# Reordering a convolution's transform stage: places of its spectra, an elementwise product, a small copy and two sets of loads

## The chip, the cores and the metric

The kernel runs on one core of one Trainium2 chip. TensorE (PE), VectorE (DVE), ScalarE (ACT) and GpSimd (POOL) compute; SyncE (SP) issues most of the DMAs and ScalarE and GpSimd issue some. The metric is the device time of one execution in microseconds, as a median of several runs.

## The reference

The output holds two computations side by side, in bfloat16. Part A is attention with a memory that runs through 64 segments in sequence; each segment needs the memory rows that the one before it put out:

```python
for s in range(n_seg):                     # 64 segments of 32 rows, D = 1024, 32 heads of 128
    h = jnp.concatenate([mem, xs], axis=1) # 8 memory rows and 32 rows of x
    q, k, v = (einsum('btd,dhe->bhte', h, W) for W in (Wq, Wk, Wv))
    ...
    o = jnp.einsum('bhte,hed->btd', o, Wo)
    mem = o[:, :M, :].copy()
```

Part B is a long convolution of u (2048 rows of 1024 channels) with a kernel K that a state space model gives:

```python
K = jnp.einsum('dn,dnl,dn->dl', Cc, P, dB).real
...
Yf = Uf * Kf                               # transforms of length 4096
y = irfft2(Yf)[..., :L]
y = y + u * Dskip
```

## The kernel before, in words

Part B is computed first (to about 594 us of 1935) and part A after it. Part A needs 512 KB tiles of weights; those that stay in SBUF are loaded while part B still computes, into places that part B has given up, and the others are streamed through a few buffers in every segment.

The changed lines lie in the stage of part B that follows the kernel's construction, the transform. The order of instructions is written out by hand (there is no scheduler): each engine executes its own instructions in program order and waits for others by semaphores. The stage is the loop `for b in range(16)` (L1530). b stands for a quarter of the channels, `dq = b // 4` (256 channels), and one of four blocks of frequencies, `kc = b % 4`. In each iteration:

- `pointwise(b)` (L1458) multiplies the transformed u by the spectrum of K. On DVE: four products `times_u` (L1381, 128x1024 float32; u comes from the buffer wq, the spectrum from PSUM, and the results go to z and back to PSUM), four `rotate` (L1384 and L1385) and the difference `od` (L1471) and sum `y` (L1472). On POOL: the spectra to be inverted, `Bt`, from y (L1474, twice) and from od (L1476 and L1477, on DVE for b = 15). `spectra` (L1454) says in which place of two tiles, Bp with eight places and Bq with four, each goes. Bp's order is the list `stay_` (L1451), which is the fourth row of PLACES.
- `load_u(b + 1)` (L1214) has SP issue the two loads of the next iteration's u into wq (L1216), each of which waits for the products that read that buffer before.
- At b = 3 and from b = 4 on, `load_pair` (L1484) has SP load rows of the plain u (tile uu, 256 KB, four buffers): pair b - 2 in iteration b, and pairs 0 and 1 in b = 3.
- PE computes the next iteration's spectrum (L1225, two halves of 20 matmuls), and behind each half one of the two inverses of pair b - 4 (L1493 to L1525): 16 matmuls of Bt with the inverse matrices MI (L1513), at some places one more with the last tap's rows (L1511), and one with the identity that adds uu (L1525). ACT evicts the sum into uu (L1526) and issues the output DMA (L1498) when both halves are there.
- `skips(n)` (L1488) multiplies uu by D (L1491) in place. That has to be done before L1525 of the same pair. It is called for pair b - 3 on POOL in iterations 3 to 14, behind POOL's spectra, and for pairs 12 to 15 on DVE after the loop.
- SP loads MI in b = 0 to 3 (L1573), in b = 2 the last tap's row, once for each of four partitions and each half of the channels (L1578), and the first rows of u (L1579). Then `next(resident)` issues one load of a part A weight (`residents`, L1674, through L268), as often as a table by b says (L1585). The places and their order are a list of dead tiles.
- At b = 3, `first_state` (L1715) loads the first segment's rows and memory; at the end of b = 10 PE transposes the memory (L1723), DVE copies the result to hT (L1724, 128x64), and POOL copies the rows (L1725).

After the loop come pair 11, three inverses that were begun, and the last eight inverses, pairs 12 to 15. The buffers of MI become free one after another, and weights are loaded into them; part A's first matmuls (L414) follow on PE, with tiles that SP's streaming fetches bring (wst, L340 and L352; a_half, L352).

In the compiled program, DMA issues of SP and ScalarE take eight semaphores in turn, so that an issue waits for the landing of the one eight before it.

Of the kernel before, what the change touches and what calls it, by code (L numbers as in the profile page):

```python
# [690 lines left out]
PLACES = ("e0 o0 e1 o1 e2 o2 e3 o3", "s0 s1 s2 s3 e0 e1 e2 e3", "o0 o1 o2 o3 s0 s2 e0 e2", "s1 s3 e1 e3 o0 o2 s0 e0")  # L691
# [21 lines left out]
def part_b(ctx, tc, u, A_re, A_im, B_re, B_im, C_re, C_im, log_dt, Dskip, out_b, ahead, copies, residents, first_state):  # L713
# [734 lines left out]
    def blocks(t_):  # L1448
        return t_.rearrange("p i c d -> p (i c) d")

    stay_ = PLACES[3].split()  # L1451
    Bp, Bq = (p.tile([128, n_, 2, 2, DQ], BF16, name="Bt", tag="B") for p, n_ in ((bp, 8), (bp0, 4)))

    def spectra(dq, kc, odd_):  # L1454
# [33 lines left out]
    def skips(n_, eng):  # L1488
        d = slice(DQ * (n_ // 4), DQ * (n_ // 4) + DQ)
        uu = held[n_][:].rearrange("p i a d -> p (i a) d")  # L1490
        eng.tensor_tensor(out=uu, in0=uu, in1=Dsk[:, d].unsqueeze(1).to_broadcast([128, 4, DQ]), op=ALU.mult)  # L1491
# [38 lines left out]
    for b in range(16):  # L1530
        points = pointwise(b, now)
        next(points)
        if 0 < b < 15:
            load_u(b + 1)
        for _ in range(4 if b in (2, 3) else 0):
            second.pop(0)()
        if b == 2:
            ks.append([])
        if 2 <= b < 6:
            lo, hi = b - 2, min(b - 1, 3) if b < 5 else 5  # L1540
            ks[1].extend(load_k(1, k1[:, DH * lo:DH * hi], lo))
        if b >= 4:
            load_pair(b - 2, iv)
        if b == 3:
            v.tensor_scalar(out=ident[:], in0=ident[:], scalar1=float(PLEN / 2), scalar2=None, op0=ALU.mult)
            load_pair(0, iv)
            load_pair(1, iv)
            state = first_state(g0[0:8, 5120:6144], iv.tile([128, 8, 24], BF16, name="xt0", bufs=1))
            next(state)
            ctx_k.close()  # L1550
            ps_h = ctx.enter_context(tc.tile_pool(name="b_psh", bufs=1, space=PSUM))
            ps_y = ctx.enter_context(tc.tile_pool(name="b_psy", bufs=2, space=PSUM))
        if b == 0:
            now = nxt_
        elif b + 1 < 16:
            now = []
            for n_ in range(2):
                if b < 3:
                    if n_:
                        next(points, None)  # L1560
                    weighted(b + 1, n_, amps[b + 1])
                now.append(halves(ps_h if b > 2 and (2 * b + n_) % 3 == 0 else ps_e))
                spectrum(b + 1, n_, [now[n_][0][:, half] for half in range(2)])
                if b == 1:
                    make(3, 7)
                if b >= 4:
                    inverses(b - 4, n_)
        next(points, None)
        if 3 <= b < 15:
            skips(b - 3, gp)  # L1570
        if b < 4:
            for i in (2 * b, 2 * b + 1):
                sy.dma_start(out=MI[i][:], in_=MId[2 * i:2 * i + 2].rearrange("c p a k q -> p c a k q"))  # L1573
        if b == 2:
            rows4 = g0[0:4, 5120:6144]
            for i in range(4):
                for half in range(2):
                    sy.dma_start(out=rows4[i:i + 1, DH * half:DH * half + DH], in_=Kx[half][31:32, NF - 1].rearrange("i g c -> i (g c)"))  # L1578
            sy.dma_start(out=w4, in_=u[0:4, :])  # L1579
            gp.tensor_tensor(out=w4, in0=rows4[:, 0:D], in1=w4, op=ALU.mult)  # L1580
            gp.memset(l4, 0.0)
            gp.memset(l4[:, :, 127:128], float(PLEN / 2))
            gp.affine_select(out=l4[:, :, 127:128], in_=l4[:, :, 127:128], compare_op=ALU.is_ge, fill=0.0, base=0, pattern=[[1, 4], [0, 1]],
                             channel_multiplier=-1)
        for _ in range({1: 2, 2: 2, 3: 1, 4: 2, 5: 2, 6: 3, 7: 2, 8: 1, 9: 1, 11: 3, 12: 3, 13: 2, 14: 3, 15: 3}.get(b, 0)):  # L1585
            next(resident)
        if b == 10:
            state.send(ps_y.tile([128, 8, 128], BF16, name="yp", tag="yp")[:, :, 0:8])
# [9 lines left out]
    for _ in range(4):  # L1598
        next(resident)
    for n_ in range(8):  # L1600
        if n_ % 2 == 0:
            skips(12 + n_ // 2, v)
        inverses(12 + n_ // 2, n_ % 2)
        if n_ == 1:
            next(state)
        next(resident)
# [31 lines left out]
@with_exitstack  # L1638
def kernel(
    ctx: ExitStack,  # L1640
    tc: tile.TileContext,
    A_x: bass.AP,
    A_mem0: bass.AP,
    A_Wq: bass.AP,
    A_Wk: bass.AP,
    A_Wv: bass.AP,
    A_Wo: bass.AP,
    A_seg_len: bass.AP,
    B_u: bass.AP,
    B_A_re: bass.AP,  # L1650
    B_A_im: bass.AP,
    B_B_re: bass.AP,
    B_B_im: bass.AP,
    B_C_re: bass.AP,
    B_C_im: bass.AP,
    B_log_dt: bass.AP,
    B_Dskip: bass.AP,
    out: bass.AP,
):
    seg_len = int(A_seg_len)  # L1660
    Dm = A_x.shape[2]
    Db = B_u.shape[2]
    out_a = out[0, :, 0:Dm]
    out_b = out[0, :, Dm:Dm + Db]
    src = weight_blocks(A_Wq.rearrange("d h e -> d (h e)"), A_Wk.rearrange("d h e -> d (h e)"),
                        A_Wv.rearrange("d h e -> d (h e)"), A_Wo.rearrange("h e d -> (h e) d"))
    WD, copies = streamed_copies(ctx, tc, src)
    ahead = Ahead(ctx, tc, A_x[0], src, seg_len)
    ctx_w = ctx.enter_context(ExitStack())
    W_res, places, first = {}, [], {}  # L1670
    rest = Keys(RESIDENT)
    rest.ctx = ahead.ctx = ctx_w

    def residents(stay, early, uqs, last):  # L1674
        def put(t_):
            load_resident(tc, None, src, rest.pop(0), W_res, None, t_)
        for _ in range(EARLY[0]):
            load_resident(tc, stay, src, rest.pop(0), W_res)
            yield
        def some(where, tag, n):  # L1680
            t_ = where.tile([128, n, 2048], BF16, name="W%d" % n, tag=tag)
            return [t_[:, i, :] for i in range(n)]
        for t_ in some(stay, "KT1", 2):
            put(t_)
            yield
        for t_ in early:
            put(t_)
            yield
        put(last[0])
        yield  # L1690
        for t_ in uqs:
            put(t_)
            yield
        ahead.wst = ctx_w.enter_context(tc.tile_pool(name="a_wst", bufs=1, side="right"))
        pool = ctx_w.enter_context(tc.tile_pool(name="a_wre0", bufs=1, side="right"))
        for _ in range(EARLY[1]):
            load_resident(tc, pool, src, rest.pop(0), W_res)
            yield
        for i, key in enumerate([("k", 0, 7)] + streamed_keys()[0:SLOTS - 1]):
            first[key] = t_ = ahead.wst.tile([128, 2048], BF16, name="wst", tag="w%d" % i)  # L1700
            tc.nc.sync.dma_start(out=t_[:], in_=WD[key][:] if key in WD else src(key))
            yield
        for i in [c // 2 for c in PAIRS]:
            places.append(lambda i=i: stay.tile([128, 2048], BF16, name="W1", tag="MI%d" % i))
        for i in range(LATE):
            put(places.pop(0)())
            yield
        put(last[1])
        yield

    low = low_blocks(ctx, tc)
    ahead.low = low.pop()
    copies += [lambda t_=t_: load_resident(tc, None, src, rest.pop(0), W_res, None, t_) for t_ in low]

    def first_state(m0, xt):  # L1715
        nc = tc.nc
        consts = constants(tc, ahead)
        hT = next(consts)
        nc.sync.dma_start(out=xt[:].rearrange("p k r -> p (k r)"), in_=ahead.VXd[0, :, 256:])
        nc.sync.dma_start(out=m0, in_=A_mem0[0])  # L1720
        pm = yield
        for kc in range(8):
            nc.tensor.transpose(out=pm[:, kc, :], in_=m0[:, kc * 128:(kc + 1) * 128], identity=ahead.consts[0][0:8, 0:8])  # L1723
        nc.vector.tensor_copy(out=hT[:, :, ahead.XM:], in_=pm)  # L1724
        nc.gpsimd.tensor_copy(out=hT[:, :, 0:ahead.XM], in_=xt[:])  # L1725
        yield
        next(consts)
        yield

    with ExitStack() as ctx_b:  # L1730
        part_b(ctx_b, tc, B_u[0], B_A_re, B_A_im, B_B_re, B_B_im, B_C_re, B_C_im, B_log_dt, B_Dskip, out_b, ahead, copies, residents, first_state)
    with ExitStack() as ctx_a:
        part_a(ctx_a, tc, A_x[0], src, WD, A_Wo.shape[0] * A_Wo.shape[1], seg_len, out_a, ahead, W_res, rest, places, first)
# [35 lines left out]
```

## Time and profile before

| | us |
|---|---|
| three runs, median (lowest to highest) | 1935.62 (1935.48 to 1936.25) |
| profiled execution, its own time | 1936.64 |
| its span, first to last instruction | 1934.9 |
| part B's transform loop and last inverses | about 407 to 594 of the span |
| PE busy over the span | 1782.2 |
| DVE busy | 1348.0 |
| ACT busy | 918.6 |
| POOL busy | 506.4 |

Rows of the profile name an engine, a line (L12 is line 12 of the kernel), an operation and its tiles as out<-in. A table by windows gives, for each stretch of the span, the busy time of each engine with the number of its instructions, then the granted clock of TensorE (1.00 is full speed), the mean busy share of the 16 DMA engines and the bytes that they moved. A row of waits gives the engine and line that waited, what ended the wait, and total, times and longest. In a list of instructions, [2.56 <-DMA wq<-Ud] is idle time of that engine just before the instruction, with what ended it. SPq and ACTq are the queues in which those engines issue DMAs; a row of the chain that ended last gives start and length of one step.

### The profile page before, as it was taken

Reading aid. Unit: us, or ns where it says so; the run is one execution under the profiler, and the core shown is the slowest. Engines: PE = TensorE matmul, PEld = TensorE weight load, DVE = VectorE, ACT = ScalarE, POOL = GpSimd, SP = SyncE. Lnnn points to the kernel's source line nnn. Section 1 sums busy time; section 2 is a strip of 40 time slices with the busy share of each in tenths; the row PEclk is TensorE's granted clock in tenths of the full one; section 3 lists DMA queues with packets and bytes.
Section 4 is the critical chain, followed back from the end, with each engine's and each line's share of the span. In section 5 each row is a group of like instructions: output and inputs, shape, how many; then the busy total and the mean of one; then the engine's idle time right before and its main releaser. Section 6 shows DMA issues by size and latency. Waiting matters only on the chain.

```text
span 1934.9 us, 73686 instructions
## 1 busy us (share of the span) xinstructions
PE 1782.2 (92%) x31512; PEld 1093.5 (57%) x31563; DVE 1348.0 (70%) x3369; ACT 918.6 (47%) x1654; POOL 506.4 (26%) x897
## 2 busy tenths in 40 slices
PE   8999999877886999999999999999999999999988
PEld 3666666546763555555555555555555555555544
DVE  8599989868992666666766676766666666666650
ACT  8799989940112343444444444434343444444420
POOL 2354545326761111111212121111111111111120
PEclk8999999878997999999999999999999999999999
DMA  7889897858789999999999999999999999999993
GB/s 221 246 235 281 234 286 235 235 171 275 226 290 358 336 346 336 331 346 344 354 347 345 342 352 336 347 344 339 329 352 339 334 344 349 345 334 342 343 336 95
DMA packets 341744, 594.21 MB, mean 307 GB/s; under 512 B 94100, under 2 KB 216476, under 8 KB 339368
## 3 DMA queue, kind: packets, MB, share of 16 engines
q1 hardware_dynamic: 297944, 534.99, 81.1%
q10 hardware_dynamic: 36816, 29.59, 4.7%
q0 software_dynamic: 6656, 24.92, 3.4%
q8 instruction: 247, 4.05, 0.8%
q14 instruction: 81, 0.66, 0.1%
HBM read 531.92 MB, written 71.63 MB: 312 GB/s over the span
## 4 chain that ended last, share of the span: by engine, by line
PE 49%; DMA 29%; DVE 12%; ACT 4%; POOL 3%; issue 3%; SPq 0%; POOLq 0%; DVEq 0%; ACTq 0%
PE acc L414 21%; DMA wst<-WD_v 11%; PE pp L527 9%; DMA wst<-WD_o 8%; DMA arena<-PKd 3%; PE pe L667 3%; DMA wst<-WD_k 3%; PE tr L425 2%; PE pro L184 2%; PE pa L1225 2%; DVE nr L1270 2%; PE pro L197 1%; PE pv L495 1%; POOL uu L1491 1%; PE ptt L1248 1%
## 5 line engine op out<-in xcount | busy, mean ns | idle before, releaser
L414 PEld LDWEIGHTS <-a_hT 128*32 128x32 bf16 x12351 | 331.4, 96 | 323.7 <-issue 75.4
L420 ACT CAST arena<-acc 128x512 bf16<-128x512 f32 x384 | 224.8, 585 | 401.2 <-PE acc L414 333.2
L527 PEld LDWEIGHTS <-arena 128*32 128x32 bf16 x8256 | 215.8, 96 | 77.9 <-issue 56.4
L414 PE MATMUL acc<-wst,a_hT 128*32 128x512 bf16 x2308 | 230.4, 383 | 31.5 <-DMA wst<-WD_v 26.0
L428 POOL COPY arena<-arena 128x128 bf16<-128x128 bf16 x128 | 37.4, 292 | 698.8 <-DMA arena<-PKd 331.4
L335 DVE TENSOR_SCALAR arena<-keep 128x256 int32<-128x256 int32 x508 | 174.3, 395 | 28.1 <-PE acc L414 28.0
L414 PE MATMUL acc<-XM,a_hT 128*32 128x512 bf16 x2560 | 184.2, 380 | 0.0
L414 PE MATMUL acc<-W,a_hT 128*32 128x512 bf16 x1536 | 133.4, 385 | 0.3 <-issue 0.3
L454 DVE TENSOR_REDUCE a_mx<-sc 128x4 f32<-128x160 f32 (+1 forms) x192 | 71.8, 374 | 78.7 <-PE sc L442 78.7
L197 PE MATMUL pro<-XM,wsl 128*128 128x512 bf16 x480 | 117.7, 383 | 5.6 <-DVE kst L206 2.2
L527 PE MATMUL pp<-W_o,arena 128*32 128x256 bf16 x3584 | 121.5, 273 | 0.9 <-issue 0.8
L544 DVE COPY arena<-tr 128x512 bf16<-128x512 bf16 x64 | 27.2, 425 | 125.9 <-PE tr L425 125.9
L458 ACT ACTIVATE sc<-sc 128x160 f32<-128x160 f32 (+1 forms) x192 | 63.9, 333 | 103.5 <-DVE sc L455 102.7
L462 DVE TENSOR_REDUCE a_mx<-sc 128x4 f32<-128x160 f32 (+1 forms) x192 | 72.6, 378 | 55.3 <-ACT sc L458 55.0
L414 PE MATMUL acc<-W_q,a_hT 128*32 128x512 bf16 x1536 | 108.3, 380 | 0.0
L489 POOL TENSOR_TENSOR arena<-arena,a_BD 128x128 bf16<-128x128 bf16 x128 | 51.0, 399 | 216.8 <-DVE arena L472 209.2
L1270 DVE TENSOR_SCALAR nr<-ptt 128x456 f32<-128x456 int16 x128 | 80.3, 628 | 31.4 <-PE ptt L1248 28.6
L1262 ACT ACTIVATE E<-pa 128x648 bf16<-128x648 f32 x128 | 87.7, 712 | 17.7 <-PE pa L1254 15.7
L527 PE MATMUL pp<-wst,arena 128*32 128x256 bf16 x1536 | 76.1, 274 | 18.8 <-DMA wst<-WD_o 16.4
L623 ACT CAST arena<-pp 128x128 bf16<-128x128 f32 x64 | 17.0, 265 | 156.3 <-DVE arena L623 156.3
L513 ACT CAST arena<-pv 128x512 bf16<-128x512 f32 (+1 forms) x128 | 61.3, 479 | 62.9 <-PE pv L499 33.0
L425 PEld LDWEIGHTS <-arena 128*128 128x128 bf16 x1024 | 57.9, 98 | 55.6 <-ACT arena L420 28.9
(332 smaller groups left out, 3961.7 us busy)
## 6 DMA issues: line engine op xcount, KB each, us to landing
wst<-WD_v SPq DMA_DIRECT2D x256, 512.0 KB
wst<-WD_k SPq DMA_DIRECT2D x192, 512.0 KB
wst<-WD_o SPq DMA_DIRECT2D x192, 512.0 KB
wst<-WD_q SPq DMA_DIRECT2D x128, 512.0 KB
Ud<-ux POOLq DMA_DIRECT2D x16, 1024.0 KB, 8.0
wq<-Ud SPq DMA_DIRECT2D x32, 512.0 KB
wsl<-in_A_Wk_dram SPq DMA_DIRECT2D x16, 512.0 KB
wsl<-in_A_Wv_dram SPq DMA_DIRECT2D x16, 512.0 KB
```

The lines of the kernel that those rows point to most:

```text
L197: nc.tensor.matmul(a[:], lhsT=w[:, kc, 128 * j:128 * j + 128], rhs=xTl[:, kc, :, :].rearrange("p s k -> p (s k)"), start=(kc == 0), stop=( ...
L335: nc.vector.tensor_scalar(out=out.bitcast(I32), in0=in_.bitcast(I32), scalar1=0, scalar2=None, op0=ALU.bitwise_or)
L414: nc.tensor.matmul(a[32 * g:32 * g + 32, o_:o_ + rhs.shape[1]], lhsT=hT[:, kc, :], rhs=rhs, start=(kc == 0), stop=(kc == KC - 1), tile_pos ...
L420: nc.scalar.copy(out=q, in_=a[:])
L425: nc.tensor.transpose(out=p[:, hl, :, :].rearrange("p a b -> p (a b)"), in_=q[:, 128 * hl:128 * hl + 128], identity=ident[:])
L454: nc.vector.tensor_reduce(out=m_, in_=x, axis=AX.X, op=ALU.max)
L458: nc.scalar.activation(out=flat(sc, i), in_=flat(sc, i), func=ACT.Exp, scale=scale)
L462: nc.vector.tensor_reduce(out=m_, in_=x, axis=AX.X, op=ALU.add)
L513: copy(out=o[:, i:i + n], in_=p[:, i:i + n, :].rearrange("p a (g q) -> p a g q", g=4))
L527: nc.tensor.matmul(po[32 * qt:32 * qt + 32, o_:o_ + rhs.shape[1]], lhsT=oT[:, h % 4, (h % 16) // 4, :], rhs=rhs, start=False, stop=(h == 3 ...
L1262: sc.activation(out=T["E", r, e // 4][:, lo:lo + 8 * NE].rearrange("p (i c) -> p i c", i=2), in_=T.pop(("p", r, e))[:, :, 0:4 * NE], func= ...
L1270: v.tensor_scalar(out=T["n", r, e // 4][:, lo:lo + 8 * NT], in0=T.pop(("t", r, e))[:, 0:8 * NT].bitcast(I16)[:, 0:16 * NT:2], scalar1=floa ...
```

## The change

The list `stay_` is written out, with s0 two places earlier. `skips` is called for pair b - 2 on POOL in iterations 4 to 14 and for pairs 0 and 1 in iteration 3, so that pair 12 comes to POOL and DVE keeps 13 to 15. The last tap's row is loaded by two DMAs that each write four partitions from one row. The table of kept weights counts 1, 1, 1, 1, 1, 2, 2, 2, 3, 2 for b = 1 to 10 in place of 2, 2, 1, 2, 2, 3, 2, 1, 1, 0, and is the same from 11 on; the tiles and their order are the same. ScalarE copies the state in place of DVE.

```diff
-    stay_ = PLACES[3].split()
+    stay_ = "s1 s3 s0 e3 e1 o0 o2 e0".split()
...
         next(points, None)
-        if 3 <= b < 15:
-            skips(b - 3, gp)
+        for n_ in (0, 1) if b == 3 else (b - 2,) if 3 < b < 15 else ():
+            skips(n_, gp)
...
         if b == 2:
             rows4 = g0[0:4, 5120:6144]
-            for i in range(4):
-                for half in range(2):
-                    sy.dma_start(out=rows4[i:i + 1, DH * half:DH * half + DH], in_=Kx[half][31:32, NF - 1].rearrange("i g c -> i (g c)"))
+            for half in range(2):
+                sy.dma_start(out=rows4[:, DH * half:DH * half + DH], in_=Kx[half][31, NF - 1].rearrange("g c -> (g c)").partition_broadcast(4))
...
-        for _ in range({1: 2, 2: 2, 3: 1, 4: 2, 5: 2, 6: 3, 7: 2, 8: 1, 9: 1, 11: 3, 12: 3, 13: 2, 14: 3, 15: 3}.get(b, 0)):
+        for _ in range({1: 1, 2: 1, 3: 1, 4: 1, 5: 1, 6: 2, 7: 2, 8: 2, 9: 3, 10: 2, 11: 3, 12: 3, 13: 2, 14: 3, 15: 3}.get(b, 0)):
             next(resident)
...
     for n_ in range(8):
-        if n_ % 2 == 0:
+        if n_ > 0 and n_ % 2 == 0:
             skips(12 + n_ // 2, v)
         inverses(12 + n_ // 2, n_ % 2)
...
-        nc.vector.tensor_copy(out=hT[:, :, ahead.XM:], in_=pm)
+        nc.scalar.copy(out=hT[:, :, ahead.XM:], in_=pm)
```

## The prediction

> **What bounds it now.** The edits touch the transform (about 405 to 594 us) and the weight loads that run beside it. I read the stretch in tables by window first, then what each engine waited for between 440 and 595 us, then single instructions.
>
> ```profile
> core 0: us, PE busy (x) PEld busy (x) DVE busy (x) ACT busy (x) POOL busy (x), PEclk, DMA share, GB/s
> 435.00:455.00 20.00, 15.68 (x112) 11.72 (x110) 16.97 (x20) 1.66 (x4) 12.88 (x14) 0.83 0.68 223
> 455.00:475.00 20.00, 15.65 (x120) 12.26 (x118) 17.28 (x20) 1.79 (x3) 10.12 (x7) 0.91 0.97 313
> 475.00:515.00 40.00, 34.61 (x296) 28.92 (x300) 39.31 (x43) 4.78 (x8) 29.44 (x22) 1.00 0.86 277
> 515.00:535.00 20.00, 17.39 (x154) 14.25 (x154) 16.96 (x20) 2.39 (x4) 13.10 (x11) 1.00 0.56 166
> 535.00:575.00 40.00, 32.07 (x263) 26.06 (x266) 38.96 (x42) 4.78 (x8) 28.35 (x21) 0.97 0.92 306
> 575.00:595.00 20.00, 19.21 (x161) 14.12 (x165) 5.74 (x6) 5.35 (x9) 12.29 (x46) 0.97 0.84 281
> 595.00:640.00 45.00, 28.73 (x517) 15.38 (x513) 16.82 (x48) 11.53 (x24) 3.09 (x9) 0.77 1.00 362
> ```
>
> DVE is busy 39.31 of 40 us and 38.96 of 40 us in two of these rows; POOL is not (29.44). From 595 on DMA is (share 1.00). So VectorE sets the pace up to its last product at 575 us, then PE's last inverses, then the transfers. What DVE waits for is short, and it is nearly all there is to win:
>
> ```profile
> DVE z L1381 <- DMA wq<-Ud: 4.9, 2, 2.6
> DVE a_hT L1724 <- PE yp L1723: 2.7, 1, 2.7
> DVE uu L1491 <- DMA uu<-in_B_u_dram: 1.4, 1, 1.4
> DVE od L1471 <- POOL uu L1491: 0.5, 1, 0.5
> ```
>
> The columns are total, times, longest. PE's own list for 440 to 640 us begins otherwise:
>
> ```profile
> PE yp L1525 <- POOL uu L1491: 17.8, 11, 3.6
> PE acc L414 <- DMA a_half<-in_A_Wq_dram: 11.0, 1, 11.0
> ```
>
> The 17.8 us is the idle time at which "u times D two inverses ahead" aims. In a steady iteration it is cover, not cost: two first products of DVE, one iteration apart, stand 9.65 us apart, and DVE has no gap between them:
>
> ```profile
> 503.93 1.21 DVE L1381 TENSOR_TENSOR z<-wq,pa 128x1024 f32<-128x1024 f32 x1
> ...
> 513.58 1.21 DVE L1381 TENSOR_TENSOR z<-wq,pa 128x1024 f32<-128x1024 f32 x1
> ```
>
> **The change part by part.**
>
> *Order of the spectra's places.* The same eight names in the same tile, another index. The instructions and what they wait for stay; no engine gets or loses one. 0, and I see no way to a loss but a changed overlap with weights that are loaded into that tile's place at the end, which come after the last inverse in both. 0 to +0.3.
>
> *Tap rows by two loads, and weights later, before b=4.* SyncE issues these one after another in b=2 and 3:
>
> ```profile
> 439.83 5.69 SPq L1578 DMA_DIRECT2D g<-Kx  x8
> ...
> 446.27 0.43 SPq L268 DMA_DIRECT2D W_q<-in_A_Wq_dram  x1
> 446.80 1.04 SPq L1216 DMA_DIRECT2D wq<-Ud  x2
> ```
>
> DVE's instructions around that load, and the loads themselves in the chain that ended last:
>
> ```profile
> 441.71 1.22 DVE L1381 TENSOR_TENSOR pa<-wq,pa 128x1024 f32<-128x1024 f32 x1
> ...
> 449.44 1.22 DVE L1472 TENSOR_TENSOR y<-y,pa 128x1024 f32<-128x1024 f32 x1
> 453.22 1.22 DVE L1381 TENSOR_TENSOR z<-wq,pa 128x1024 f32<-128x1024 f32 x1 [2.56 <-DMA wq<-Ud]
> ...
> 461.74 1.22 DVE L1472 TENSOR_TENSOR y<-y,pa 128x1024 f32<-128x1024 f32 x1
> ```
> ```profile
> 446.80 6.33 DMA wq<-Ud
> ...
> 457.71 7.54 DMA wq<-Ud
> ```
>
> Eight tap rows hold SP for 5.69 us (0.71 each); two hold it for about 1.4. One of the two weights behind them goes too (0.4 with its gap). So SP reaches the load of u (L1216) at about 442.1, and then waits for the product that still reads its buffer, which ends at 441.71+1.22 = 442.93. It is issued 3.85 us earlier. With an unchanged 6.33 us it lands at 449.3, before DVE is free at 449.44+1.22 = 450.66. The 2.56 us go. The second half (issued at 447.3, and now about 446.65, behind b=3's second product) is wanted 2.26 us after the first; one weight fewer ahead of it, 512 KB or 1.45 us at the 362 GB/s of the last window row, makes it timely; if that helps nothing it costs 0.85 again. **−2.56 (−1.7 to −2.56).**
>
> *The same, b=5.* The second wait (4.9 less 2.56) ends with the load issued at 457.71, which took 7.54 and landed at 465.25; DVE had been free since 461.74+1.22 = 462.96. With the first wait gone that is 460.4. SP comes there earlier too, at about 454.5 (−3.2: it loses the first delay and one more weight), so 0.65 is won with the same duration, and up to all 2.38 if two weights fewer (three before b=4 instead of five; 2.9 us at 362 GB/s) shorten the 7.54 fully. They don't: the kept queue is full only in part of that time (share 0.97 for 455 to 475), and MI and W_q stay ahead. I take the middle, **−1.6 (0 to −2.38)**, leaving 0.8 of wait.
>
> *Weights moved to b=6 to 10.* Counts 3,2,1,1,0 become 2,2,2,3,2: the same 16 by b=10. In b=9 (from 503.93) and 10 (from 513.58) the queue then carries 5 tiles instead of 1, 2.1 MB more, 5.8 us at 362 GB/s, in stretches whose shares are 0.86 and 0.56, which leave 5.6 and 8.8 us. Iterations with three tiles exist already (b=11, 12, 14) and lie in the row with share 0.92, where DVE stays at 38.96 of 40 us. **0; if one load of u came late there, about +2.5, like the two waits above.**
>
> *State's copy on ScalarE.* DVE's instruction waits in order for PE's transposes:
>
> ```profile
> 522.08 1.22 DVE L1472 TENSOR_TENSOR y<-y,pa 128x1024 f32<-128x1024 f32 x1
> 526.00 0.19 DVE L1724 COPY a_hT<-yp 128x64 bf16<-128x64 bf16 x1 [2.69 <-PE yp L1723]
> 526.10 1.21 DVE L1381 TENSOR_TENSOR z<-wq,pa 128x1024 f32<-128x1024 f32 x1
> ```
>
> Without it the product starts at 522.08+1.22 = 523.30 instead of 526.10: **−2.8**. Next late would be its PSUM input from PE or the second half of u. PE has 17.39 of 20 us in that window, so its spectrum can be the next wait, at most some tenths: −2.2 to −2.8. ScalarE takes the copy beside 2.39 us of work in 20; behind it wait one eviction and one output DMA, by 2.7 us at most, which no product of DVE needs. 0.
>
> *u times D earlier.* POOL gets one more, of DVE's four, and does two in b=3:
>
> ```profile
> L1491 POOL TENSOR_TENSOR uu<-uu,Dsk x12: 2116/2127/2136, 457.5 to 570.2; 128x1024 bf16<-128x1024 bf16 x12
> ```
> ```profile
> 490.06 0.38 SPq L1486 DMA_DIRECT2D uu<-in_B_u_dram  x1
> ```
> ```profile
> 457.51 2.13 POOL L1491 TENSOR_TENSOR uu<-uu,Dsk 128x1024 bf16<-128x1024 bf16 x1 [1.54 <-DMA uu<-in_B_u_dram]
> ...
> 494.44 2.50 POOL L1474 TENSOR_TENSOR Bt<-y 128x512 bf16<-128x512 f32 x2 [2.53 <-DVE y L1472]
> ...
> 499.36 2.14 POOL L1491 TENSOR_TENSOR uu<-uu,Dsk 128x1024 bf16<-128x1024 bf16 x1
> ```
>
> The extra 2.13 us on POOL in b=3 stand in its idle time before b=4's spectra; 0. In the loop POOL's place for it does not move, but it takes the pair whose load was issued in the same iteration: 490.06 to 499.36 is 9.3 us for a load for which POOL waited once already (at 457.51). PE's 17.8 us vanish; DVE gains of them only the wait of 0.5 at b=13 (taken 0, −0.5 to +0.3).
>
> In the tail they count, since DVE is done:
>
> ```profile
> 572.35 0.38 PE L1525 MATMUL yp<-uu,b_ident 128*128 128x512 bf16 x1 [3.11 <-POOL uu L1491]
> ```
> ```profile
> 574.84 3.32 POOL L1474 TENSOR_TENSOR Bt<-y 128x512 bf16<-128x512 f32 x2 [2.54 <-DVE y L1472]
> ```
> ```profile
> 599.96 8.70 DMA a_half<-in_A_Wq_dram
> ```
>
> PE comes to its last eight inverses 3.11 earlier, but cannot pass POOL's last spectra (578.16); I count 2.3 us. Of these little arrives: the next part waits 11.0 us for a_half, whose 8.70 us in a full queue follow an issue by SP, and SP stood before a weight load for most of this:
>
> ```profile
> SPq L268 <- DMA out_dram<-uu: 10.4, 2, 9.0
> ```
>
> In this program an issue from SP or ScalarE waits for the landing of the one eight issues before it, whose semaphore it takes; here that was an output. After it, landings are set by the bytes queued since DVE's end, which move with DVE. **−0.8 (0 to −4.6)** for the part of PE's 2.3 that frees W1's places and outputs sooner.
>
> **Sum.** −2.56 −1.6 −2.8 −0.8 = −7.8 us against the profiled run (span 1934.9, 1936.64 with what lies around it): 1928.8. The median of three is 1.02 lower, so **1927.8**. It carries to the end because DMA is full from 595 on, and moving the start of a full queue moves its end.
>
> **Rivals.**
>
> 1. *The queue is the bound already.* If the transform's loads fill the time, an earlier DVE only meets a later load. For it: shares of 0.97, 0.92, 0.84. Against: 0.56 and 0.86 leave 14 us before 535, and the weights by b=10 are as many in both. It would leave the first wait's saving and little else: −3, 1932.6.
> 2. *Loads of u stay late.* b=5 keeps its 2.38 (−6.2, 1929.4), and one of the refilled iterations gets a wait of 2.5: −3.7, 1931.9.
> 3. *The tail carries through.* If outputs land sooner, SP's 9.0 us of waiting shortens, and with it the idle share of DMA before 595 (0.84 of 20 us, 3.2 us idle): 2.3 more, up to 4.6: 1923.2 to 1925.5. Against: the 9.0 us are one output's, with SP's queue full beside it, and that queue is as full in the changed kernel. The Trainium skill (DMA: Bandwidth & Descriptors, Queues, rings and completion order) says that each DMA engine takes packets in turn from the queue rows that have work, so that ScalarE's output should not wait behind all of SP's transfers; by that rule the time would be this rival's. The trace does not agree with it, by those 9.0 us.
> 4. *PE's chain is the truth.* All 17.8 us go: −18 and the rest, 1917 or less. Against: DVE has no gap in a steady iteration.
> 5. *Slower: the load of the pair comes too late for POOL.* POOL does its work in order; u times D stands ahead of the next spectra, which free od and y for DVE. It is asked 9.3 us after issue; POOL then has 2.5 us of idle time (the wait at 494.44). DVE's next od gives another 2.2: it starts 7.25 after its iteration's first product (522.08−1.25−513.58), so at 501.5 in the iteration that began at 494.3, when POOL had read the last od by 499.36. From 14.0 us of transfer on, each us more costs 1 us in each of 11 iterations; at 15.1 that is 11.7: +3.9, 1939.5. Against: 7.54 and 8.70 are the long transfers of these rows.
>
> **How the numbers follow.** Forecast 0.52 (its own range 1925.3 to 1929.9, half of the way from the terms taken to the sums of their ends, −3.6 and −12.8), rival 1: 0.11, rival 2: 0.15 (a third of it the later waits), rival 3: 0.14, rival 4: 0.03, rival 5: 0.05. 0.2%, about what a measurement of this kernel can tell from no change, is 3.9 us: below 1931.75 is faster. Rival 1 and a third of rival 2 are within it: 0.16; slower 0.05; faster 0.79. The range 1923.2 to 1932.7 leaves out rivals 4 and 5 and the edges of 1 and 3, under 0.2.
>
> **What would show it.** In the profile after: DVE's list without L1724 and with 0.8 us or less before L1381; PE's 17.8 us for L1491 gone, without any change of DVE's 9.65 us; first product of b=15 about 7 us earlier; a_half landing about 8 us earlier; the rest of the program shifted alike. Wrong it is if POOL waits for DMA before L1491 in the loop, if L1381 waits for wq at b=10 to 15, or if a_half's landing moves by much less than DVE's end.

## The result, and the profile after

The changed kernel takes 1927.82 us in the median of 16 runs (1918.85 to 1939.08), the kernel before 1934.3 in 16 runs beside it (1926.73 to 1942.21). The ratio is 0.9963, with a 95% interval of 0.9947 to 0.998: 7.2 us less, from 3.9 to 10.3. The forecast was 1927.8, 7.8 us below the 1935.62 of the first three runs before.

From lowest to highest the executions of one kernel lie 15 to 20 us apart, so the parts can't be read from times. They can be read from one profile each, since the loop's steps repeat within some hundredths of a microsecond. The profiled execution after has a span of 1924.1 us (its own time is 1925.86). The windows of before, in the changed kernel (columns as there):

```profile
475.00:515.00 40.00, 36.49 (x315) 30.23 (x314) 39.31 (x42) 4.78 (x8) 29.61 (x22) 1.00 0.87 277
515.00:535.00 20.00, 18.63 (x164) 15.05 (x163) 19.66 (x22) 2.49 (x5) 15.08 (x12) 1.00 0.92 305
535.00:575.00 40.00, 34.14 (x278) 27.08 (x277) 37.66 (x40) 6.11 (x11) 29.16 (x32) 0.97 0.90 289
575.00:595.00 20.00, 14.58 (x148) 9.93 (x146) 1.98 (x3) 4.04 (x7) 6.20 (x32) 0.93 1.00 351
```

The third busy time is DVE's: the hole of b = 11 (16.96 of 20 us before) is closed, 19.66. From 475 to 515 DVE is as full as before; from 535 to 575 it has 37.66 in place of 38.96, since its last y now comes 6 us earlier. DMA's share from 575 to 595, 0.84 before, is 1.00. The waits of DVE in the loop and the tail (total, times, longest):

```profile
DVE z L1381 <- DMA wq<-Ud: 2.2, 1, 2.2
DVE uu L1491 <- issue: 1.0, 1, 1.0
DVE uu L1491 <- DMA uu<-in_B_u_dram: 0.8, 1, 0.8
```

One of two waits for u has stayed, nearly whole; L1724 and od at b = 13 are gone. Of PE's waits, 440 to 640 us, these are the ones to compare:

```profile
PE acc L414 <- DMA a_half<-in_A_Wq_dram: 10.7, 1, 10.7
PE pa L1225 <- DVE y L1385: 9.1, 10, 1.6
...
PE yp L1525 <- POOL uu L1491: 0.2, 1, 0.2
```

17.8 us of waiting for u times D became 0.2, and the waiting for DVE (L1385), which frees the PSUM that the spectrum is written to, grew from 1.8 to 9.1.

To cut the stretch into parts I use three starts of DVE's last instruction of an iteration, L1472 (y of b = 2, 5 and 15), and the first matmul that waits for a_half. Before, then after; the last row of each is PE's:

```profile
438.58 1.22 DVE L1472 TENSOR_TENSOR y<-y,pa 128x1024 f32<-128x1024 f32 x1
...
473.85 1.22 DVE L1472 TENSOR_TENSOR y<-y,pa 128x1024 f32<-128x1024 f32 x1
...
573.54 1.22 DVE L1472 TENSOR_TENSOR y<-y,pa 128x1024 f32<-128x1024 f32 x1
...
608.70 0.61 PE L414 MATMUL acc<-a_half,a_hT 128*32 128x512 bf16 x2 [10.96 <-DMA a_half<-in_A_Wq_dram]
```
```profile
438.53 1.22 DVE L1472 TENSOR_TENSOR y<-y,pa 128x1024 f32<-128x1024 f32 x1
...
471.02 1.22 DVE L1472 TENSOR_TENSOR y<-y,pa 128x1024 f32<-128x1024 f32 x1
...
567.48 1.22 DVE L1472 TENSOR_TENSOR y<-y,pa 128x1024 f32<-128x1024 f32 x1
...
600.32 0.61 PE L414 MATMUL acc<-a_half,a_hT 128*32 128x512 bf16 x2 [10.74 <-DMA a_half<-in_A_Wq_dram]
```

The differences in us, with the same rows of each experiment's profile (one profile each; E6, E7 and E11 were also timed in 10 or 12 runs):

| kernel | y2 to y5 | y5 to y15 | y15 to a_half | sum |
|---|---|---|---|---|
| before | 35.27 | 99.69 | 35.16 | 170.12 |
| changed | 32.49 | 96.46 | 32.84 | 161.79 |
| E1: before, copy on ScalarE | 35.38 | 96.46 | 35.45 | 167.29 |
| E2: before, two tap loads | 32.69 | 99.67 | 35.68 | 168.04 |
| E3: before, new table of weights | 33.36 | 99.67 | 35.44 | 168.47 |
| E4: before, u times D earlier | 35.93 | 98.04 | 33.17 | 167.14 |
| E5: changed, old order of places | 32.60 | 96.46 | 32.94 | 162.00 |
| E6: changed, two MI later | 30.16 | 96.45 | 32.90 | 159.51 |
| E7: changed, pairs loaded last | 32.99 | 96.46 | 33.59 | 163.04 |
| E8: changed, u times D late | 32.50 | 96.46 | 35.61 | 164.57 |
| E9: before, outputs held | 35.31 | 101.15 | 33.17 | 169.63 |
| E10: changed, outputs held | 32.89 | 96.46 | 31.45 | 160.80 |
| E11: changed, MI later, outputs held | 31.91 | 96.46 | 32.14 | 160.51 |
| E12: changed, old table of weights | 33.16 | 96.44 | 33.37 | 162.97 |

The change moved 8.33 us in this stretch: 2.78, 3.23 and 2.32. What follows a_half, 1326.2 us before (1934.9 less 608.70) and 1323.8 after, holds the same instructions in both, and in these 14 profiles it varies from 1319.6 (E2) to 1329.6 (E11) without order. The y of b = 2 stands at 436.93 (E4) to 442.44 (E9). These two are the spread of the times.

### The profile page after: what moved, and what is told of

Its sections match the earlier page's. It is cut to its first block, busy times and chain, and to the rows that moved or that the text cites. A ratio compares the mean times of both kernels' runs of the same rounds, so it can differ in the third digit from the quotient of the medians.

```text
span 1924.1 us, 73734 instructions
## 1 busy us (share of the span) xinstructions
PE 1779.6 (92%) x31563; PEld 1091.4 (57%) x31563; DVE 1346.2 (70%) x3367; ACT 919.5 (48%) x1655; POOL 508.2 (26%) x898
## 4 chain that ended last, share of the span: by engine, by line
PE 45%; DMA 32%; DVE 14%; ACT 4%; issue 3%; POOL 2%; SPq 1%; DVEq 0%; POOLq 0%; ACTq 0%
PE acc L414 21%; DMA wst<-WD_v 12%; PE pp L527 8%; DMA wst<-WD_o 8%; DMA wst<-WD_k 3%; PE pe L667 3%; DMA arena<-PKd 2%; DMA wst<-WD_q 2%; PE tr L425 2%; DVE nr L1270 2%; PE pro L184 1%; PE pro L197 1%; PE pv L495 1%; PE pa L1225 1%; DVE gr L1236 1%
## 5 line engine op out<-in xcount | busy, mean ns | idle before, releaser
L414 PEld LDWEIGHTS <-a_hT 128*32 128x32 bf16 x12351 | 329.3, 96 | 333.8 <-issue 81.9
L414 PE MATMUL acc<-wst,a_hT 128*32 128x512 bf16 x2308 | 230.7, 382 | 40.5 <-DMA wst<-WD_v 31.8
L414 PE MATMUL acc<-XM,a_hT 128*32 128x512 bf16 x2560 | 184.1, 380 | 0.0
L414 PE MATMUL acc<-W,a_hT 128*32 128x512 bf16 x1536 | 133.5, 385 | 0.0
L197 PE MATMUL pro<-XM,wsl 128*128 128x512 bf16 x512 | 122.7, 383 | 3.4 <-DVE kst L206 2.2
L414 PE MATMUL acc<-W_q,a_hT 128*32 128x512 bf16 x1536 | 108.1, 379 | 0.0
```

The source lines that it names most:

```text
L197: nc.tensor.matmul(a[:], lhsT=w[:, kc, 128 * j:128 * j + 128], rhs=xTl[:, kc, :, :].rearrange("p s k -> p (s k)"), start=(kc == 0), stop=( ...
L414: nc.tensor.matmul(a[32 * g:32 * g + 32, o_:o_ + rhs.shape[1]], lhsT=hT[:, kc, :], rhs=rhs, start=(kc == 0), stop=(kc == KC - 1), tile_pos ...
```

## The experiments

**E1, the copy alone.** Before, with

```diff
-        nc.vector.tensor_copy(out=hT[:, :, ahead.XM:], in_=pm)
+        nc.scalar.copy(out=hT[:, :, ahead.XM:], in_=pm)
```

> The kernel before with one edit: ScalarE makes the state's copy. Read in the profile, not from the time, since single executions of a kernel differ by several us. Theory (DVE sets the pace until its last product, and a shift of it arrives whole at the first segment): DVE's 2.7 us of waiting at L1724 go, its last y (L1472, 573.5 before) starts 2.8 us earlier, and the first matmul on a_half (608.7 before) also 2.8 (2.2 to 3.2) earlier. Rival (the transfers' queue is the bound): y moves by 2.8, the a_half matmul by less than 1.

The loop from y5 to y15 is 3.23 us shorter: 2.9 at b = 11 and the 0.36 of od at b = 13, which went with it. From y2 to a_half 2.83 are left. An earlier DVE does arrive at part A; the queue of transfers doesn't eat it, as the theory had it.

**E2, the two tap loads alone.**

```diff
-            for i in range(4):
-                for half in range(2):
-                    sy.dma_start(out=rows4[i:i + 1, DH * half:DH * half + DH], in_=Kx[half][31:32, NF - 1].rearrange("i g c -> i (g c)"))
+            for half in range(2):
+                sy.dma_start(out=rows4[:, DH * half:DH * half + DH], in_=Kx[half][31, NF - 1].rearrange("g c -> (g c)").partition_broadcast(4))
```

> The kernel before with one edit: the last tap's row by two loads. Theory (SP's issue is what made the load of u late): DVE's wait of 2.56 us at b = 4 falls to 1.0 or less, since that load is then issued when the products that read its buffer end, about 443, with two weights still ahead of it; last y 1.6 to 2.6 us earlier, unless b = 5 takes some back. Rival (the queued weights made it late): the wait stays over 1.5 us.

y2 to y5 falls from 35.27 to 32.69, almost all that the whole change gives (32.49), with both weights still ahead of the load. The wait at b = 4 is gone, the one at b = 5 is there (2.44; the load of u and PE's L1513 end it within 0.1 us of each other). SP's time at the tap loads was the cause, as the theory had it; what SP does in that time stands in the section on the prediction.

**E3, the table of weights alone.**

```diff
-        for _ in range({1: 2, 2: 2, 3: 1, 4: 2, 5: 2, 6: 3, 7: 2, 8: 1, 9: 1, 11: 3, 12: 3, 13: 2, 14: 3, 15: 3}.get(b, 0)):
+        for _ in range({1: 1, 2: 1, 3: 1, 4: 1, 5: 1, 6: 2, 7: 2, 8: 2, 9: 3, 10: 2, 11: 3, 12: 3, 13: 2, 14: 3, 15: 3}.get(b, 0)):
```

> The kernel before with one edit: the table of kept weights. Theory: with eight tap rows SP still reaches b = 4's load of u only at about 446.4, one weight less ahead of it in the queue; the wait of 2.56 us falls by 1.3 us or less; b = 5's wait stays over 1.5 us, as it does in the changed kernel (2.24). Last y 0 to 1.5 us earlier. No wait for a load of u appears at b = 9 to 12. Rival (the weights are the cause of both waits): both fall below 0.5, last y 4 to 5 us earlier.

1.9 us: 1.6 at b = 4 (0.96 of waiting is left) and 0.3 at b = 5, where 2.07 stay. A little over the theory at b = 4, far from the rival. The weight ahead of the load is thus a second cause of the wait at b = 4 while the eight tap loads are there: either edit alone shortens it. No wait for u at b = 9 to 12.

**E4, u times D earlier, alone.**

```diff
-        if 3 <= b < 15:
-            skips(b - 3, gp)
+        for n_ in (0, 1) if b == 3 else (b - 2,) if 3 < b < 15 else ():
+            skips(n_, gp)
...
-        if n_ % 2 == 0:
+        if n_ > 0 and n_ % 2 == 0:
```

> The kernel before with one edit: u times D two inverses ahead. Theory: PE's 17.8 us of waiting for L1491 go; DVE's last y moves by 0.5 us only (the wait of od at b = 13); PE's last inverses end (first L414 matmul, 594.3 before) 2 to 2.7 us earlier, and the a_half matmul 1.5 to 2.7 us earlier. Rival (PE's chain of uu is what bounds the loop): last y 5 us or more earlier, a_half likewise. Rival (tail gain is eaten by the queue): a_half under 0.7 earlier.

The tail is 1.99 us shorter, within the theory, though PE's last inverses end only 1.0 us sooner after the last y (first L414 matmul at 590.73), under the theory's 2 to 2.7. The loop is 1.65 us shorter, which neither had: at b = 11 the transposes that DVE's copy waits for come sooner. They stand behind inverses in PE's order, and PE no longer loses time there to uu. DVE's row:

```profile
523.37 0.19 DVE L1724 COPY a_hT<-yp 128x64 bf16<-128x64 bf16 x1 [1.07 <-PE yp L1723]
```

1.07 in place of 2.69. So two parts of the change remove the same wait, and their single gains don't add. The other steps of the loop stay 9.64 us, but for b = 13 (10.00), where od's wait stays, against the theory. Rival 4, under which the 17.8 us bound the loop, falls. From y2 to y5 E4 is 0.66 us longer, with longer waits for u (5.6 us in place of 4.9).

**E5, the changed kernel with the old order of places.**

```diff
-    stay_ = "s1 s3 s0 e3 e1 o0 o2 e0".split()
+    stay_ = PLACES[3].split()
```

> The changed kernel with the old order of the spectra's places. Theory: nothing moves; last y (567.5 in the changed kernel) and the a_half matmul (600.3) within 0.4 us. Rival (the order of addresses lets something start earlier): one of them moves by 1 us or more.

Each part within 0.11 us of the changed kernel. The order does nothing that these profiles show.

**E6, what b = 5 waits for.** The changed kernel, with the last two tiles of MI behind the load of u:

```diff
-        if b < 4:
-            for i in (2 * b, 2 * b + 1):
+        if b < 3 or b == 4:
+            for i in (2 * b, 2 * b + 1) if b < 3 else (6, 7):
```

> The changed kernel with one edit: the last two tiles of the inverse matrices (MI 6 and 7, first needed at b = 7) are loaded at the end of b = 4 in place of b = 3, so behind b = 5's load of u. Theory (b = 5's wait of 2.24 us is the queue ahead of that load, of which MI is 3.3 us): the wait goes, last y 2.2 us earlier (565.2), a_half matmul 1.8 to 2.4 us earlier (598.2); about 0.1% faster than the changed kernel, 0.5% faster than the kernel before. Rival (it is the load's own length, or the wait passes on to b = 6): last y moves by less than 1 us.

y2 to y5 is 30.16, 2.33 less, with steps of 9.65 us at b = 4 and b = 5: the wait is gone and doesn't pass on. MI's place costs in two ways that this run doesn't part: b = 5's load is also issued 1.5 us sooner (at 454.20, 14.38 us after b = 2's y, in place of 15.92). The starts themselves moved less than expected (y15 at 566.43), because b = 2's y stands 1.3 us later in this execution (439.82); the differences don't carry that. Time: 0.9945 of before (0.992 to 0.9969), in 12 runs; the interval overlaps the changed kernel's, so it is not shown to be faster than that.

**E7, the price of a late pair.** The changed kernel; load and product of the pair come behind the weights:

```diff
-        if b >= 4:
-            load_pair(b - 2, iv)
...
-        for n_ in (0, 1) if b == 3 else (b - 2,) if 3 < b < 15 else ():
+        for n_ in (0, 1) if b == 3 else ():
             skips(n_, gp)
...
+        if b >= 4:
+            load_pair(b - 2, iv)
+            if b < 15:
+                skips(b - 2, gp)
         if b == 10:
```

> The changed kernel, but each pair of u (uu) is loaded at the end of its iteration, behind the kept weights in SP's queue, and multiplied right after: the load is issued later and has 1 to 3 tiles of 512 KB more ahead of it. Theory (POOL's idle time of 2.5 us and od's 2.2 cover late loads): where three weights are issued POOL waits up to some us before L1491, DVE's od waits only where the load lands over 4.7 us late; last y 0 to 4 us later than the changed kernel's, the time 0 to 0.2% over it. Rival (each us that POOL waits is paid): last y later by the whole of POOL's waits, 10 us or more.

POOL now waits, five times:

```profile
POOL uu L1491 <- DMA uu<-in_B_u_dram: 3.2, 5, 1.0
```

and y5 to y15 is 96.46 to the hundredth. What POOL loses lies in its own idle time, so the rival's price is not paid. y2 to y5 is 0.50 us longer than in the changed kernel (the last section has a cause), and the tail 0.75, whose cause is open. Time: 0.9964 (0.9934 to 0.9994), as the changed kernel.

**E8, the changed kernel with u times D late** (E4's edit undone).

> The changed kernel with u times D back to one inverse ahead (pair b - 3 on POOL, pairs 12 to 15 on DVE). Theory: last y as in the changed kernel, 0.5 us later at most; PE's waits of some 18 us for L1491 come back; first L414 matmul and the a_half matmul 2 to 2.7 us later (588.3 and 602.5). Rival (the tail's gain comes from the earlier DVE alone, or from the weights): a_half within 0.7 us of the changed kernel.

The loop is unchanged, 96.46, though PE waits again 12.8 us for L1491; the tail is 2.77 us longer. So the tail's gain is that of u times D, whatever DVE and the weights do: all kernels with u times D late and the outputs not held have a tail of 35.16 to 35.68, all with it early 32.84 to 33.59. Beside the copy on ScalarE u times D has no other gain.

**E9 and E10, the tail.** Outputs of pairs 12 to 15 behind the last weight load, in the kernel before and in the changed one:

```diff
+    outs = []
     for n_ in range(8):
...
         inverses(12 + n_ // 2, n_ % 2)
+        if n_ % 2:
+            outs.append(ended.pop())
...
-    while ended:
-        ended.pop(0)()
     for _ in resident:
         pass
+    for put in outs:
+        put()
```

> The kernel before, with the outputs of pairs 12 to 15 issued together after the last weight load of part B, so that no weight load of SP waits for one of them. Theory (SP's stop of 9.0 us on an output, and the gap in the transfers that follows, is what the earlier u times D shortens): SP's wait on out_dram in that stretch is under 1.5 us, and the time from DVE's last y to the a_half matmul, 35.2 us before and 32.8 in the changed kernel, falls to 31.5 or less: 2 us for the gap and about 2 for three outputs of 256 KB that no longer go ahead of it. Rival (only the bytes ahead count): it falls by 2 us or less, to 33.0 or more.

> The changed kernel with the same edit. Theory: its stop on an output (5.4 us) left 1 us or less of gap, so the time from the last y to the a_half matmul falls from 32.8 by the three outputs and that: 2 to 3 us, to about 30. The outputs follow behind, so the end gains 1 us at most. Rival (PE, whose work is no earlier, sets it): within 0.7 us of 32.8.

E9 fell from 35.16 to 33.17, E10 from 32.84 to 31.45: 2.0 and 1.4 us, less than the theory's numbers, and E9 lies on the rival's side of the line that was drawn (33.0). SP still stops on outputs in E9's tail, 4.0 us in two stops at L268, where the theory had under 1.5 us. And both numbers of the theory took it that the outputs would no longer go ahead of a_half, but they do. In E9 ScalarE issues them first, and then SP a_half (two views of one kernel):

```profile
599.67 2.77 ACTq L1498 DMA_DIRECT2D out_dram<-uu  x4
```
```profile
605.16 0.80 SPq L352 DMA_DIRECT2D a_half<-in_A_Wq_dram  x1
```

The gap in the transfers is to be seen in windows after the last y (15 to 25 us behind it); the last two columns are DMA's share and GB/s. Before, changed, E9:

```profile
588.54:592.54 4.00, 3.95 (x34) 3.11 (x34) 0.00 (x0) 0.99 (x2) 0.68 (x4) 1.00 1.06 384
592.54:594.54 2.00, 2.00 (x19) 1.16 (x20) 0.00 (x0) 0.32 (x2) 0.00 (x0) 1.00 0.41 109
594.54:596.54 2.00, 2.00 (x44) 1.01 (x40) 1.29 (x2) 0.74 (x2) 0.00 (x0) 1.00 0.73 216
596.54:598.54 2.00, 1.20 (x24) 0.48 (x17) 0.00 (x0) 0.33 (x1) 0.00 (x0) 1.00 0.90 274
```
```profile
586.48:588.48 2.00, 2.00 (x44) 0.98 (x40) 1.29 (x2) 0.74 (x2) 0.00 (x0) 1.00 1.01 281
588.48:590.48 2.00, 1.10 (x24) 0.42 (x13) 0.00 (x0) 0.23 (x1) 0.00 (x0) 1.00 0.80 220
590.48:592.48 2.00, 0.00 (x0) 0.00 (x0) 0.00 (x0) 0.00 (x0) 0.00 (x0) 1.00 1.05 400
```
```profile
597.90:599.90 2.00, 2.00 (x21) 1.11 (x22) 0.00 (x0) 0.32 (x2) 0.00 (x0) 1.00 1.05 387
599.90:601.90 2.00, 2.00 (x45) 0.97 (x40) 1.29 (x2) 0.31 (x1) 0.00 (x0) 1.00 1.05 347
601.90:603.90 2.00, 1.02 (x20) 0.41 (x13) 0.00 (x0) 0.00 (x0) 0.00 (x0) 1.00 1.00 281
```

Idle shares of 0.59, 0.27 and 0.10 of 2 us are 1.9 us before; 0.4 in the changed kernel; none in E9. So this hole does close. That its closing is the gain is not shown, though. From the last y to the a_half matmul as a whole (before, changed, E9), DMA's share and rate are nearly the same:

```profile
573.54:608.70 35.16, 23.41 (x212) 16.43 (x212) 9.12 (x10) 5.96 (x10) 12.45 (x46) 0.84 0.91 317
567.48:600.32 32.84, 18.88 (x169) 12.38 (x167) 8.49 (x9) 5.37 (x9) 11.97 (x46) 0.84 0.92 320
578.90:612.07 33.17, 23.24 (x216) 16.54 (x215) 9.01 (x10) 5.99 (x11) 12.53 (x46) 0.91 0.92 319
```

That is 3.2, 2.6 and 2.7 us of idle share in all, only about 0.5 us less, and 11.1, 10.5 and 10.6 MB moved (time by rate). Most of the gain goes with fewer bytes moved before a_half lands; which transfers those are was not tried. Holding the outputs doesn't let SP issue a_half earlier either. In E9 that comes 26.26 us after the last y (26.42 before), and the transfer is shorter, 6.86 us in place of 8.70:

```profile
605.16 6.86 DMA a_half<-in_A_Wq_dram
```

In E10 it comes 27.18 us after the last y (24.01 in the changed kernel) and takes 4.22 us in place of 8.79. So E9 and E10 show that the outputs' place in the order is worth 1.4 to 2.0 us, and not by which path. E9's loop is 1.5 us longer at b = 14, where DVE waits for loads of u (L1381, 0.99 and 0.29 us); why was not tried, and only its tail is used.

**E11, both.** E6's and E10's edits in the changed kernel.

> The changed kernel with the two tiles of MI later (as in the experiment with MI) and the outputs held. Theory: DVE without the wait at b = 5, last y minus b = 2's y 126.6 us (129.0 in the changed kernel), and the tail as in the experiment before; the a_half matmul 4 to 5 us earlier than in the changed kernel, of which the end keeps 2.5 to 3.5: 0.994 to 0.995 of the kernel before. Rival (streaming in part A absorbs it): 0.996 or more.

0.9936 of before (0.9917 to 0.9955), 1923.94 us in 12 runs against 1933.71. This is the lowest ratio, but its interval overlaps the changed kernel's (0.9947 to 0.998), so it is not shown to be faster than that. The a_half matmul came only 1.3 us nearer to b = 2, not 4 to 5: y2 to y5 is 31.91 and not 30.16, for a reason that the last section has, and the tail won 0.7. The ratio came out a little below the 0.994 to 0.995 of the theory while the stretch moved a third of what it said, so the ratio doesn't confirm it.

**E12, the changed kernel with the old table of weights.** E3's edit undone.

> The changed kernel with the old table of kept weights (2, 2, 1, 2, 2, 3, 2, 1, 1, 0 for b = 1 to 10). Theory (the two tap loads alone removed b = 4's wait, and the later weights did nothing for b = 5): from b = 2's y to b = 5's 32.5 us as in the changed kernel (32.49), within 0.5; from there to the last y 96.5; no wait at b = 4. Rival (the later weights carry part of it): 1 us or more longer from b = 2 to b = 5, with a wait for wq at b = 4 or a longer one at b = 5.

33.16, 0.67 over the changed kernel: between the two, nearer to the theory. There is no wait at b = 4, and b = 5 waits 0.99, not longer. In this profile the load of u for b = 5 is issued at 455.67, 16.31 us after b = 2's y (15.92 in the changed kernel), and takes 8.24 us (7.96). The later issue comes from b = 3, from the same cause as in E11: DVE's product that frees the buffer ends later. The longer transfer may be the weights' or not: E7 and E8, which have the new table and the same delay at b = 3, have 32.99 and 32.50. In E2, which has the old table without that delay, the transfer took 7.98 and y2 to y5 is 0.20 longer than in the changed kernel. So of the gain at b = 4 and 5 the later weights have a few tenths at most, once the tap loads are two. The tail is 0.53 us longer, which I can't explain.

## Why the prediction was right, and where it was wrong

The time was right to the microsecond, more by luck than the sum deserves: two terms were off by 1.5 us each, with opposite signs, and the kernel before, from whose 1935.62 the sum was taken, has 1934.3 in the longer measurement. Of the signs that were named, a_half came 8.38 us earlier (about 8 forecast) and the last y 6.06 (about 7 for b = 15's first product), but DVE's wait before L1381 is 2.2 and not 0.8 or less.

- *DVE is the bound of the loop.* Right. y5 to y15 is 96.44 to 96.46 in each kernel without the copy on DVE, whether PE waits for uu (E1, E8) or not, and whether POOL waits for the pair (E7) or not. PE's 17.8 us were cover, all but the part of them that made DVE's copy wait at b = 11 (E4).
- *b = 4, −2.56.* Right in size (the step went from 12.30 to 9.64 us), and it was SP that made the load late (E2). But the sum read SP's 5.69 us as the time to issue eight loads, 0.71 each. In 3.5 us of them SP waits: the eight loads take all eight semaphores, and three of them wait for the landing of an issue eight before, two of MI and one of k. SP's waits at these loads before, and the two loads in the changed kernel:

```profile
SPq L1578 <- DMA MI<-MId: 2.0, 2, 1.1
SPq L1578 <- DMA k<-Kx: 1.5, 1, 1.5
```
```profile
439.78 0.76 SPq L1577 DMA_DIRECT2D g<-Kx  x2
```

  Two loads hold SP for 0.76 us, and not for 1.4. The weight that I let leave the queue was not needed for it, though alone it takes 1.6 us off (E3).
- *b = 5, −1.6.* Wrong: 2.38 became 2.24. The step that failed is "two weights fewer shorten the 7.54": the load was issued at 454.45, as forecast (454.5), and then took 7.96, where the sum had 7.54 or less. (The hit at 454.5 is chance too: SP's last issue before it ends at 453.74, and SP then waits for the landing of k, eight issues back.) The chain of the changed kernel there:

```profile
449.01 0.63 SPq L1088
449.64 0.04 issue
449.69 4.70 DMA k<-Kx
454.38 0.02 issue
454.40 0.02 SPq L1216
454.42 0.03 issue
454.45 7.96 DMA wq<-Ud
```

DMA's busy tenths from 449 to 456 us, 40 slices of 0.175 us, show the queue empty for moments between 450.7 and 451.5:

```profile
DMA  8665424132080026877879999999994688999999
```

While SP issues four small loads of some 0.63 us each (L1088, from 446.98 on) and one of 128 KB, the queue runs dry. Weights that were ahead of that point can't shorten anything behind it. What is ahead of the load of u is what SP issued from 450.42 on: uu twice, MI twice, one weight and two small loads. Taking MI away ends the wait (E6), taking weights away from earlier iterations doesn't (E3); with the old table the transfer took 7.98 (E2).
- *b = 9 and 10, 0 for more weights.* Right: no wait there, at a DMA share of 0.92 for 515 to 535.
- *The copy, −2.8.* Right (2.9 in E1). But the same wait was more than half due to uu (E4), which the sum didn't see; had I summed the parts as measured alone, E1, E2, E3 and E4 give 2.83, 2.08, 1.65 and 2.98, 9.5 us, for 8.33 together.
- *b = 13, 0.* 0.36 gone, within the bounds. It went with the copy (E1) and not with u times D (E4 keeps it), to which the prediction gave it.
- *The tail, −0.8.* Undersized: 2.32. The step that failed is "of these little arrives". PE's part was near the forecast: from the last y to the first L414 matmul it took 20.78 us before and 18.68 after, 2.1 us less. But a_half doesn't follow that end of PE's work: in E4 it gains 1.0 us and a_half 1.99. It follows a chain of issues in which each waits for a landing, to be seen in the chains that ended last. Before, changed, E4:

```profile
593.93 6.01 DMA W<-in_A_Wo_dram
...
599.96 8.70 DMA a_half<-in_A_Wq_dram
```
```profile
574.22 10.49 DMA out_dram<-uu
...
585.19 6.29 DMA W<-in_A_Wo_dram
...
591.49 8.79 DMA a_half<-in_A_Wq_dram
```
```profile
588.97 5.94 DMA W<-in_A_Wo_dram
...
594.93 9.10 DMA a_half<-in_A_Wq_dram
```

  The weight load (W) is issued right after SP's stop on an output, and its landing lets a_half be issued. Before and in E4 a step of PE's inverses ends within 0.5 us of that stop, so that the two can't be told apart there; in the changed kernel the output stands alone. Counted from the last y, the weight load is issued after 20.39, 17.71 and 18.07 us, and a_half after 26.42, 24.01 and 24.03; the two transfers take the same time within 0.4 us. The output of pair 12 on which SP stops is issued 6.74 us after the last y in the changed kernel (574.22) and 10.10 before (583.64). That is rival 3's mechanism, with 1.5 us more than the sum in place of its 2.3. SP's longest stop on an output fell from 9.0 to 5.4 us:

```profile
SPq L268 <- DMA out_dram<-uu: 6.4, 2, 5.4
```

  It did not go: the output above took 10.49 us to land beside SP's queue. The Trainium skill's rule that stood beside rival 3 (DMA: Bandwidth & Descriptors, Queues, rings and completion order) gets no support from that row.

- *Places, 0.* Right (E5).
- *Rival 5, slower.* POOL does wait when the load is moved behind the weights (E7), but the point from which DVE would pay for it is not reached even then.

## What to carry to other kernels

Find the engine that has no gap in a steady iteration, list what it does wait for, and price each edit by that list alone; the largest wait in the chain (here 17.8 us of PE) can be cover. To shorten a late load, look for the last moment at which its queue was empty: only what was issued after that is ahead of it. When an engine is held at its DMA issues, look at what it waits for there: in this program each issue waits for the landing of the one eight before. Such waits were 3.5 of the 5.69 us at eight small loads, and they tied a_half to the landing of an output.

## What had not been expected of the hardware

At b = 3 DVE scales the identity (L1545, 0.19 us) while POOL multiplies the tap rows (L1579). Which starts first is a matter of 0.02 to 0.23 us in eight of the nine kernels with two tap loads (0.63 in E5). The changed kernel, then E12, DVE's and POOL's views of each:

```profile
446.48 0.19 DVE L1545 TENSOR_SCALAR b_ident<-b_ident 128x128 bf16<-128x128 bf16 x1
```
```profile
446.70 2.12 POOL L1579 TENSOR_TENSOR k<-g,k 4x1024 bf16<-4x1024 bf16 x1 [1.25 <-DMA k<-in_B_u_dram]
```
```profile
447.32 2.14 DVE L1545 TENSOR_SCALAR b_ident<-b_ident 128x128 bf16<-128x128 bf16 x1
```
```profile
447.30 2.10 POOL L1579 TENSOR_TENSOR k<-g,k 4x1024 bf16<-4x1024 bf16 x1 [1.01 <-DMA k<-in_B_u_dram]
```

In all four profiles in which POOL began first (E7, E8, E11, E12), DVE's small instruction took 1.94 to 2.14 us and ended within 0.1 us of POOL's; in the ten others it took 0.19. Before, POOL began 1.0 us after DVE, since the rows of u for which it waits were issued behind the eight tap loads, so the faster loads brought this chance with them. It costs little while b = 5 waits anyway (E8: y2 to y5 as in the changed kernel), and 1.75 us in E11, where that wait is gone (31.91 less 30.16). The Trainium skill (SBUF — State Buffer, Who interferes with whom) has the rule: DVE and GpSimd share a pair of ports, a tensor_scalar on DVE can run in a mode that needs it, and the one that is first holds it for its whole instruction. The traces agree, with 0.19 against 1.94 to 2.14 us. No run here moved one of the two instructions on purpose, so the cause rests on the order of the starts in 14 profiles.
